# A fused attention and feed-forward kernel: the rounding of the remaining keys moves to ScalarE, and the static order of the start is redrawn

## The chip, the cores and the metric

The kernel runs on one core of a Trainium2 chip. The metric is the device time of one execution in microseconds; the kernel before took 277.38 us in the median of three runs (276.81 to 309.06). The profile comes from one profiled execution, whose span was 274.6 us. The engines are called PE (TensorE, matmuls), PEld (its weight loads), DVE (VectorE), ACT (ScalarE), POOL (GpSimd) and SP (SyncE, which issues nearly all of the transfers).

## The reference

Two blocks follow each other: a polynomial-sketch attention, and a multiplicative feed-forward network on its output.

```python
# q, k, v: (4 batches, 4 heads, 1088 rows, 32); S1, S2: (8, 32), held as float64
def phi(x):
    a = np.einsum('rd,bhsd->bhsr', S1, x)
    b = np.einsum('rd,bhsd->bhsr', S2, x)
    return np.einsum('bhsi,bhsj->bhsij', a, b).reshape(*x.shape[:-1], r * r)
q_p, k_p = (phi(q), phi(k))
kv = np.einsum('bhsf,bhsd->bhfd', k_p, v)
z = np.sum(k_p, axis=2)
num = np.einsum('bhsf,bhfd->bhsd', q_p, kv)
den = np.einsum('bhsf,bhf->bhs', q_p, z)[..., None] + 1e-06
attn = (num / den).astype(np.float32)
# x: the attention output as (4352, 128); w1, w2 (128, 1024), w3 (1024, 1024), w_out (1024, 128)
a = x @ w1
b = x @ w2
h = a * b @ w3
out = (h @ w_out).astype(np.float32)
```

The denominator needs more accuracy than one f32 product gives. The kernel therefore never sums `k_p` for it; it takes the Gram matrix of the keys, G = sum of k kᵀ, with every key split into a rounded leading part and a rest, and gets the denominator's matrix from S1, G and S2. That is the "Gram chain": Gram products, then `G`, then `T`, then `N`, then the query matrices `R`. The 1088 rows of a head are 8 chunks of 128 and 64 remaining rows; the "remaining keys" are those 64 rows of two batches, stacked on 128 partitions.

## The kernel before

The order of all instructions is fixed when the program is built. Steps are entered in a plan with engine, estimated time, what they read and write, and a rank; a list scheduler then emits them one after the other, lower rank first among those that could start at about the same time. `EARLY` holds the ranks of the first batch's steps, `FIRST` those of the rest, `PRODUCTS` how many small matmuls a step issues. Where the plan sees TensorE idle it inserts matmuls on zeros (`idle_ps`), which compute nothing that is used.

```python
def first_rest(m, g, engine):          # leading part of the remaining keys
    for x, t, rows in rest_rows(m):    # two groups of 64 partitions
        if engine is nc.vector:
            round_to(t[:, 0], x, g[rows])
            continue
        gb = bview(g[rows], [[0, H], [0, D]])
        engine.tensor_add(t[:, 0], x, gb)
        engine.tensor_sub(t[:, 0], t[:, 0], gb)

def second_rest(m, engine):            # what the leading part leaves
    for x, t, _ in rest_rows(m):
        engine.tensor_sub(t[:, 1], x, t[:, 0])

# first batch: "first_r": first_rest(0, g[0], nc.gpsimd), "second_r": second_rest(0, nc.gpsimd)

def G_rest():                          # end of G: PSUM to SBUF, then masked blocks
    gb = work.tile([128, D], F32, tag="gb", bufs=1, name="gb")
    nc.vector.tensor_sub(gb, acc["g1"], acc["ga"])
    nc.vector.tensor_add(gb, gb, acc["g2"])
    acc["G"].append(blocks("gB", gb))  # blocks: tensor_mul of two SBUF tiles

# ... (pair_steps, the rest of T)
    nc.vector.tensor_sub(b, hi, a); nc.vector.tensor_add(b, b, lo); nc.vector.tensor_add(s, a, b)

# ... key features of batch 0 on GpSimd, two halves, from b_sb in SBUF
op(f"kp{half}", "POOL", 1.92, f"kp{half}", (("w3c", "b", half),), (("kp", 0, half),))

# ... queries, group g (two groups of 512 rows to a batch)
def lead_q():                          # ScalarE
    nc.scalar.activation(s["q2"], s["qT"], ACT.Identity, bias=g)
    nc.scalar.activation(s["q1"], s["q2"], ACT.Identity, bias=g, scale=-1.0)
def rest_q():                          # "rem", GpSimd
    nc.gpsimd.tensor_add(s["q2"], s["qT"], s["q1"])
# split, dens, dens2, phi: VectorE work on 128x256 tiles, most of it with two SBUF inputs

# ... sums over the keys of batch b = 1, 2, 3 on TensorE (32-column tiles)
p.op("gs0", "PE", 0.75, st["gs0"], (("k", b), ("kk", b)), (("kvz", b),))
p.op("gs1", "PE", 1.1, lambda: run_all(st[x] for x in ("gs1", "rg")), ...)
p.op("kv0", "PE", 0.5, st["kv0"], (("kp", b, 0), ("v", b)), (("kvz", b),))
kv1 = p.op("kv1", "PE", 0.6, lambda: run_all(st[x] for x in ("kv1", "rv")), ...)

# ... feed-forward, group g, chunk c of 8: a = x w1 (PE), copy (ACT), b = x w2 (PE), a*b (DVE), o += ab (w3 w_out) (PE)
```

The feed-forward uses w3 and w_out multiplied together beforehand (`w3_t`, the transposes, and `w3_mm`); the raw float64 weights are turned to f32 by ACT (`cv_c`, `cv_m`, `sgn`) and DVE.

Of the kernel before, what the change touches and what calls it, by code (L numbers as in the profile page):

```python
# [27 lines left out]
def bview(t, free):  # L28
# [6 lines left out]
        "q2": 1, "ay": 1, "ayC": 1, "hl": 1, "pr": 1, "bs": 1, "pT": 1, "xT": 3, "oT": 2, "b_sb": 2}  # L35
SHARED = {"t", "wa", "wb", "ph", "kvz"}

COLUMNS = {"ay": 32, "ab": 32, "rg": 32, "rv": 32, "gs0": 32, "gs1": 32, "kv0": 32, "kv1": 32, "nd0": 64, "nd1": 64, "nd4": 16}

PRODUCTS = {"ay": 48, "ay2": 32, "ab": 16, "gs0": 64, "gs1": 76, "rg": 12, "rv": 4, "kv0": 32, "kv1": 36, "nd4": 64, "w3_mm": 16, "w3_t": 4}  # L40
MOST = 120
TURN = 0.1

FIRST = {"words": 1, "conv": 1.5, "early": 1.5, "k": 2, "KX": 10, "q": 0.8, "q_act": 1, "k_act": 0, "a": 2, "b": 2.1,
         "o": 0.9, "many": 6, "late": 3, "w3_t": 1, "w3_t_copy": 0, "w3_mm": 1.7, "k1": 1.3, "mul": 0.55, "wait": 0.35}

EARLY = {"tr": -9, "Pg": -8, "sT": -10, "grid": -8, "split": -10, "grid1": -2, "tr1": -7, "rem": -8.5, "rem1": -6,
         "lead": -10, "lead1": -6, "R": -7, "k_ab0": -11, "k_ab1": -6, "r_ab": -9, "r_tr": -9, "kv0": -12, "kv1": -5,
         "rv": -10, "P_mm": -12, "P_copy": -8, "P": -8, "kp0": -8, "kp1": -10, "r_kp": -8.5, "peak1": -8.5, "gs1": -12,
         "k_tr": -10, "rg": -11, "second_r": -9.5}  # L50

HELD = {"dens", "dens2", "conv", "second", "T_rest"}
LATENCY = {"PE": 0.27, "DVE": 0.2, "ACT": 0.23, "POOL": 0.3, "SP": 3.8}


class Plan:
# [36 lines left out]
    def order(self):  # L93
        ops = self.ops
        tiles = {tag: list(keys) for tag, keys in self.held.items()}
        end, left, res, clock = {}, [], [], {}
        columns = 128
        issued = []
        pool, held = [], (0.0, 0.0)
        turn = {}  # L100
        for op in ops:
            for key in op[5]:
                if key[0] not in SHARED:
                    turn.setdefault(key[0], []).append(key)
        for n, (_, engine, us, *_r) in enumerate(ops):
            if engine is None:
                end[n] = (None, us)
            else:
                left.append(n)

        def seen(n, engine):
            e, t = end[n]
            return t if e in (None, engine) and e != "SP" else t + LATENCY[e]

        while left:
            best = {}
            for i in left:
                _, engine, us, _, deps, new, rank = ops[i]
                if any(d not in end for d in deps):
                    continue  # L120
                t = max([clock.get(engine, 0.0)] + [seen(d, engine) for d in deps])
                ok = all(key[0] in SHARED or turn[key[0]][0] == key for key in new)
                for key in new:
                    before = tiles.get(key[0], [])
                    if len(before) >= BUFS[key[0]]:
                        users = self.users[before[-BUFS[key[0]]]]
                        if any(u not in end for u in users):
                            ok = False
                            break
                        t = max([t] + [seen(u, engine) for u in users])  # L130
                if engine == "PE" and COLUMNS.get(ops[i][0], 128) != columns:
                    t += TURN
                if engine == "PE":

                    room = MOST - PRODUCTS.get(ops[i][0], 2)
                    for at, count in reversed(issued):
                        room -= count
                        if room < 0:
                            t = max(t, at + (4.0 if 18 < at < 95 else 2.0 if at > 18 else 0.5))
                            break  # L140
                if ok:
                    best.setdefault(engine, []).append((t, rank(tiles, end) if callable(rank) else rank, i))
            first = None
            for engine, c in best.items():
                t0 = min(c)[0] + 0.1
                t, r, i = min((x for x in c if x[0] <= t0), key=lambda x: (x[1], x[2]))

                for x in c:
                    if x[0] <= t0 - 0.1 + FIRST["wait"] and x[1] < min(r, 0) - 0.9:
                        t, r, i = x  # L150
                if first is None or t < first[0]:
                    first = (t, i, engine)
            t, i, engine = first
            left.remove(i)
            us = ops[i][2]
            if engine == "DVE":
                if ops[i][0] in HELD:
                    us += 0.7 * sum(max(0.0, min(f, t + us) - max(s, t)) for s, f in pool[-2:])
                held = (t, t + us) if ops[i][0] in HELD else (t, t)
            elif engine == "POOL":  # L160
                pool.append((t, t + us))
                clock["DVE"] = clock.get("DVE", 0.0) + 0.7 * max(0.0, min(held[1], t + us) - max(held[0], t))
            end[i] = (engine, t + us)
            clock[engine] = t + us
            if engine == "PE":
                columns = COLUMNS.get(ops[i][0], 128)
                issued.append((t, PRODUCTS.get(ops[i][0], 2)))
            for key in ops[i][5]:
                tiles.setdefault(key[0], []).append(key)
                if key[0] not in SHARED:  # L170
                    turn[key[0]].pop(0)
            res.append((t, i))
        return res
# [3 lines left out]
def kernel(  # L177
# [249 lines left out]
    def run_all(steps):  # L427
        for f in steps:
            f()
# [263 lines left out]
            yield k_rs[m][rows], kk_rs[rows, i], rows  # L693

    def first_rest(m, g, engine):
        for x, t, rows in rest_rows(m):
            if engine is nc.vector:
                round_to(t[:, 0], x, g[rows])
                continue
            gb = bview(g[rows], [[0, H], [0, D]])  # L700
            engine.tensor_add(t[:, 0], x, gb)
            engine.tensor_sub(t[:, 0], t[:, 0], gb)

    def second_rest(m, engine):
        for x, t, _ in rest_rows(m):
# [2 lines left out]
    def lead_first():  # L708
# [14 lines left out]
        def second(part):  # L723
# [2 lines left out]
        chunks = lambda half: lambda t: t[:, :, 4 * half:4 * half + 4]  # L726
        return {"peak0": lambda: peak(0), "peak1": lambda: peak(1), "peaks": peaks,
                "first": first, "second0": lambda: second(chunks(0)), "second1": lambda: second(chunks(1)),
                "first_r": lambda: first_rest(0, g[0], nc.gpsimd), "second_r": lambda: second_rest(0, nc.gpsimd)}

    def lead(b):

# [195 lines left out]
    def k_ops(b):  # L928
# [19 lines left out]
            kp = op(f"kp{half}", "DVE", 1.15, (("ph", "k", b),), (("kp", b, half),), rank)  # L948
        if b == 2:
            rest_ops(m, kp)  # L950
        p.op("gs0", "PE", 0.75, st["gs0"], (("k", b), ("kk", b)), (("kvz", b),))
        p.op("gs1", "PE", 1.1, lambda: run_all(st[x] for x in ("gs1", "rg")), (("k", b), ("kk", b), ("kkr", m)), (("kvz", b),))
        p.op("kv0", "PE", 0.5, st["kv0"], (("kp", b, 0), ("v", b)), (("kvz", b),))
        kv1 = p.op("kv1", "PE", 0.6, lambda: run_all(st[x] for x in ("kv1", "rv")), (("kp", b, 1), ("v", b), ("kpr", m), ("vr", m)),
             (("kvz", b),))
        if b + 2 < B:
            for which in "kv":
                p.op("load", "SP", 2.0, lambda which=which: load_in(which, b + 2), (), ((which, b + 2),), 3)
        if b == 1:
            p.op("load", "SP", 0.7, lambda: load_rest(v_rs, v, 1, of_one), (), (("vr", 1),), 1, (kv1,))  # L960
        fin1 = op("fin1", "DVE", 1.7, (("kvz", b),), (("G", b),), rank)
        op("T_mm", "PE", 0.6, (("G", b),), (("t", "T", b),))
        op("T_pair", "DVE", 1.4, (("t", "T", b),), (("Tp", b),), rank)
# [216 lines left out]
    def q_ops(g):  # L1180
# [21 lines left out]
                p.op("load", "SP", 1.6, lambda: load_by_head("q", b + 2), (), (("qh", b + 2),), 3)  # L1202
        op("grid", "DVE", 0.35 + 0.6 * w, (qT,), (("gq", g),), after=begin)
        op("lead", "ACT", 0.2 + 1.2 * w, (qT, ("gq", g)), (("q1", g), ("q2", g)))
        op("rem", "POOL", 1.15, (qT, ("q1", g), ("q2", g)), (("q2", g),))
        R = [*(("R", b) for b in batches), *(("Rs", n) for n in range(4))]
        if lean:
            op("ay1", "PE", 0.25, (("q1", g), *(R if g else (("Rh", 0), ("Rs", 0)))), (("wa", "ay", g),), after=last_phi)
        else:
            p.op("ay", "PE", 0.12 + 1.2 * w, lambda: run_all((st["ay1"], st["ay2"])), (qT, ("q1", g), ("q2", g), *R),  # L1210
                 (("wa", "ay", g), ("wb", "ay", g)), 0, last_phi)
# [116 lines left out]
    def first_ops():  # L1328
# [19 lines left out]
        op("first", "DVE", 0.73, "first", (("k", 0), ("gk", 0)), (("kk", 0),))  # L1348
        op("second0", "DVE", 0.62, "second0", (("k", 0), ("kk", 0)), (("k2", 0),))
        op("second1", "DVE", 0.65, "second1", (("k", 0), ("kk", 0)), (("k2", 1),))  # L1350
        op("first_r", "POOL", 1.7, "first_r", (("kr", 0), ("gk", 0)), (("kkr", 0),))
        op("second_r", "POOL", 0.95, "second_r", (("kr", 0), ("kkr", 0)), (("kkr", 0),))
        for half in range(2):
            ps = ("h", "ab", half)
            op(f"k_ab{half}", "PE", 0.98, f"ab{half}", (("kT", 0, half), ("ST",)), (ps,))
# [14 lines left out]
        op("P_mm", "PE", 0.75, sketch_P_mm, (("pT", "s"),), (("wa", "P"),))  # L1370
        op("P_copy", "ACT", 0.2, sketch_P_copy, (("wa", "P"),), (("Pc",),))
        op("Pg", "DVE", 0.58, sketch_P_peak, (("Pc",),), (("Pg",),))
        op("P", "POOL", 1.93, sketch_P, (("Pc",), ("Pg",)), (("P",),))
        op("T_lead", "DVE", 0.9, "T_lead", (("t", "T"),), (("Tp", 0),))
        op("T_rest", "DVE", 0.55, "T_rest", (("t", "T"), ("Tp", 0)), (("Tb", 0),))
        op("N_mm1", "PE", 0.2, "N_mm1", (("Tp", 0), ("P",)), (("t", "N"),))
        op("N_mm2", "PE", 0.4, "N_mm2", (("Tb", 0), ("P",)), (("t", "N"),))
# [96 lines left out]
```

## Time and profile before

| what | value |
|---|---|
| time, median of 3 | 277.38 us |
| span of the profiled execution | 274.6 us |
| PE busy | 266.8 us (97%) in 2556 matmul records |
| DVE busy | 208.8 us (76%) |
| ACT busy | 122.7 us (45%) |
| POOL busy | 21.4 us (8%) in 31 instructions |
| matmuls on zeros | 55 records, 13.8 us busy |
| TensorE clock granted | 1.00 in all but the last stretch |

Busy time is the union of the records of an engine. The matmuls overlap each other in the pipeline, so the time that one adds is read from the distance between the starts of consecutive ones: the two records of one f32 128x512 product take 1.02 us in the timeline, but the next product starts 0.86 us after it. The last stages of the profile show how long the start lasts: the first feed-forward matmul starts 32.13 us into the span.

### The profile page before, as it was taken

What the parts mean: (1) busy time and instruction counts of PE and PEld (TensorE: products, weight loads), DVE (VectorE), ACT (ScalarE), POOL (GpSimd) and SP (SyncE); (2) the same over time, 40 slices, a digit from 0 to 9 for tenths busy, and PEclk for the clock granted to TensorE, in tenths of its full rate; (3) what the DMA queues carried; (4) which work ended last, traced back from release to release, by engine and by line L of the source; (5) the groups of instructions that cost most, each with busy time, mean ns of one, the idle gap of its engine ahead of it and who ended that gap; (6) DMA issues with size and microseconds to landing.
All of it is one profiled execution on the core that took longest, in us unless ns stands there. A gap on an engine that the chain in (4) does not pass through costs nothing.

```text
span 274.6 us, 6300 instructions
## 1 busy us (share of the span) xinstructions
PE 266.8 (97%) x2556; PEld 150.6 (55%) x2556; DVE 208.8 (76%) x507; ACT 122.7 (45%) x265; POOL 21.4 (8%) x31
## 2 busy tenths in 40 slices
PE   7999999998999999999999999999999999999995
PEld 2865634476774767645454446454444444444665
DVE  7999999999999999995648699847795585583231
ACT  4783977997866982111232240224123222323120
POOL 2772001000000010000010010001000100000000
PEclk9999999999999999999999999999999999999999
DMA  4759999579820210020200200020002002000103
GB/s 138 271 127 314 280 383 221 183 205 304 242 78 21 79 63 2 2 39 2 38 2 0 40 0 5 0 40 2 0 0 41 0 2 38 2 0 11 31 0 57
DMA packets 28876, 22.42 MB, mean 82 GB/s; under 512 B 20016, under 2 KB 25392, under 8 KB 28848
## 3 DMA queue, kind: packets, MB, share of 16 engines
q1 hardware_dynamic: 28704, 21.96, 29.2%
q8 instruction: 20, 0.33, 0.5%
q10 hardware_dynamic: 144, 0.07, 0.1%
q14 instruction: 8, 0.07, 0.1%
HBM read 19.80 MB, written 2.23 MB: 80 GB/s over the span
## 4 chain that ended last, share of the span: by engine, by line
PE 83%; DVE 11%; DMA 2%; ACT 2%; issue 1%; DVEq 0%; ACTq 0%
PE ps_o L1292 21%; PE b_ps L1273 19%; PE a_ps L1263 19%; PE ps_w3o L577 5%; PE ps_kvz L775 3%; PE ps_wt L565 3%; PE ps_c L1034 2%; DMA raw<-in_moe_w_dram 2%; PE idle_ps L358 2%; PE ps_o L1288 1%; PE ps_xt L1156 1%; PE ps_ab L672 1%; DVE ph L1109 1%; DVE w L424 1%; DVE qT L1173 1%
## 5 line engine op out<-in xcount | busy, mean ns | idle before, releaser
L1268 ACT COPY ffa<-a_ps 128x512 f32<-128x512 f32 (+1 forms) x72 | 40.5, 563 | 104.1 <-PE a_ps L1263 104.0
L1278 DVE TENSOR_TENSOR ab<-ffa,b_ps 128x512 f32<-128x512 f32 (+1 forms) x72 | 46.6, 649 | 41.3 <-PE b_ps L1273 38.5
L1273 PE MATMUL b_ps<-xT,w 128*128 128x512 f32 (+1 forms) x144 | 71.1, 575 | 0.0
L1263 PE MATMUL a_ps<-xT,w 128*128 128x512 f32 (+1 forms) x144 | 70.6, 572 | 0.1
L1292 PE MATMUL ps_o<-ab,w3o 128*128 128x512 f32 x128 | 65.6, 604 | 0.0
L1273 PEld LDWEIGHTS b_ps<-xT,w 128*128 128x128 f32 x144 | 26.1, 190 | 29.1 <-issue 24.3
L1263 PEld LDWEIGHTS a_ps<-xT,w 128*128 128x128 f32 x144 | 26.3, 190 | 27.2 <-issue 19.8
L1292 PEld LDWEIGHTS ps_o<-ab,w3o 128*128 128x128 f32 x128 | 22.8, 190 | 21.0 <-issue 19.0
L1007 POOL TENSOR_TENSOR q<-qT,q 128x512 f32<-128x512 f32 x8 | 9.6, 1194 | 184.9 <-ACT q L1003 181.4
L375 ACT CAST sgn<-cv_c 128x512 f16<-128x512 f32 x22 | 17.2, 782 | 0.0
L577 PE MATMUL ps_w3o<-wo,w3T 128*128 128x128 f32 x128 | 15.8, 275 | 1.0 <-issue 1.0
L577 PEld LDWEIGHTS ps_w3o<-wo,w3T 128*128 128x128 f32 x128 | 15.1, 192 | 1.6 <-issue 1.3
L358 PE MATMUL idle_ps<-zeros 128*128 128x448 bf16 x55 | 13.8, 396 | 1.8 <-DVE zeros L352 1.8
L411 ACT ACTIVATE cv_c<-raw 128x512 f32<-128x512 f32 x22 | 15.3, 696 | 0.0
L414 ACT ACTIVATE cv_m<-raw 128x512 int32<-128x512 uint32 x22 | 15.2, 692 | 0.0
L424 DVE CUSTOM_DVE_ANT_0 w3c<-w3c,cv_m 128x1024 uint16<-128x1024 uint16 x16 | 11.9, 743 | 0.4
L1109 DVE TENSOR_TENSOR ph<-ay,bs 128x512 f32<-128x512 f32 (+1 forms) x12 | 11.1, 948 | 0.2
L421 DVE SCALAR_TENSOR_TENSOR w3c<-cv_c,sgn 128x512 int32<-128x512 int32 x16 | 10.9, 683 | 0.3 <-ACT sgn L375 0.3
L565 PEld LDWEIGHTS ps_wt<-ident,w3c 128*128 128x128 f32 x64 | 7.7, 144 | 6.0 <-issue 2.8
L572 ACT COPY w3T<-ps_wt 128x512 f32<-128x512 f32 x16 | 9.5, 595 | 2.1 <-PE ps_wt L565 1.7
L358 PEld LDWEIGHTS <-zeros 128*128 128x128 bf16 x55 | 5.7, 109 | 7.7 <-issue 2.9
L565 PE MATMUL ps_wt<-ident,w3c 128*128 128x128 f32 x64 | 9.8, 276 | 0.0
(213 smaller groups left out, 354.5 us busy)
## 6 DMA issues: line engine op xcount, KB each, us to landing
raw<-in_moe_w_dram SPq DMA_DIRECT2D x20, 512.0 KB, 6.4
qh<-in_q_dram SPq DMA_DIRECT2D x4, 544.0 KB, 7.2
out_dram<-oT SPq DMA_DIRECT2D x33, 64.0 KB, 2.0
k_sb<-in_k_dram SPq DMA_DIRECT2D x4, 512.0 KB, 8.1
kh<-in_k_dram SPq DMA_DIRECT2D x12, 128.0 KB, 4.0
v_sb<-in_v_dram SPq DMA_DIRECT2D x12, 128.0 KB, 7.0
raw<-in_moe_w_out_dram SPq DMA_DIRECT2D x2, 512.0 KB, 7.4
v_sb<-in_v_dram SPq DMA_DIRECT2D x1, 512.0 KB, 5.1
```

What stands on the lines that cost most here:

```text
L358: nc.tensor.matmul(ps[:, :448], zeros[:, :128], zeros, start=True, stop=True)
L375: nc.scalar.copy(bview(t.bitcast(F16)[:, 1:], [[2, n]]), c)
L411: nc.scalar.mul(x["c"], halves(raw[n], CW)[1].bitcast(F32), 2.0 ** -112)
L414: nc.scalar.mul(x["m"].bitcast(I32), halves(raw.pop(n), CW)[0].bitcast(U32), 2.0 ** -29)
L424: nc.vector.tensor_tensor(x["t"], x["t"], x["m"].bitcast(I32), ALU.add)
L565: nc.tensor.transpose(ps[i][:, c], w3c[i][:, c * 128:(c + 1) * 128], ident)
L577: nc.tensor.matmul(ps["mm"], w3T[ko][:, c], wo[:, c], start=(c == 0), stop=(c == NC - 1))
L1263: nc.tensor.matmul(a_sb[g, c, "ps"][:, :n], w1[:, c * 128:(c + 1) * 128], xT[key], start=True, stop=True)
L1268: nc.scalar.copy(a_sb[g, c][:, :n], a_sb.pop((g, c, "ps"))[:, :n])
L1273: nc.tensor.matmul(ab_sb[g, c, "ps"][:, :n], w2[:, c * 128:(c + 1) * 128], xT[key], start=True, stop=True)
L1278: nc.vector.tensor_mul(ab_sb[g, c][:, :n], a_sb.pop((g, c))[:, :n], ab_sb.pop((g, c, "ps"))[:, :n])
L1292: nc.tensor.matmul(o_ps[g][:, :n], w3o[:, c], ab_sb.pop((g, c))[:, :n], start=c == 0, stop=c == NC - 1)
```

## The change

It does five things, all for the order in which the start and the key sums run:

1. The leading part of the first batch's remaining keys is rounded by ScalarE (one negation of the grid and four activations with a bias) instead of GpSimd (two additions and two subtractions).
2. The ranks of the first batch's steps are redrawn so that the Gram products come before the key features on TensorE, and the sketch matrix P before the key features on GpSimd; the second query group's peak goes behind the first group's `phi`.
3. The second query group's rest (`rem`) may start only after its first product `ay1`, which puts it beside `split` instead of beside the first group's `phi`.
4. For batches 2 and 3 the Gram sums are one step, and the key-value sums are one step, so that nothing is put between their halves.
5. The plan's own rules change: three more VectorE steps count as held up by GpSimd, the limit on small matmuls is dropped after 95 us of planned time, and `FIRST` ranks `b` before `o`.

The rest of the diff makes the list scheduler itself faster on the host and changes no instruction.

```diff
-PRODUCTS = {..., "gs0": 64, "gs1": 76, ...}
+PRODUCTS = {..., "gs": 140, "kv": 68, "gs0": 64, "gs1": 76, ...}
-FIRST = {..., "a": 2, "b": 2.1, "o": 0.9, ..., "w3_t_copy": 0, ...}
+FIRST = {..., "a": 2, "b": 1.9, "o": 1.95, ..., "w3_t_copy": 0.3, ...}
-EARLY = {..., "sT": -10, "grid1": -2, "tr1": -7, "rem": -8.5, "lead": -10, "k_ab0": -11, "k_ab1": -6, "r_ab": -9,
-         "kv0": -12, "P": -8, "kp0": -8, "kp1": -10, "k_tr": -10, "second_r": -9.5, ...}
+EARLY = {"first_r": -13, "k_tr_copy": -12.5, ..., "sT": -9.2, "grid1": -7, "tr1": -7.5, "rem": -11, "lead": -11,
+         "k_ab0": -6, "k_ab1": -5.9, "r_ab": -5.5, "kv0": -5, "P": -12, "kp0": -5, "kp1": -5, "k_tr": -12,
+         "second_r": -12, "gs0": -12, "b_copy": -9, "ay2": -10, "ay1": -11, ...}
-HELD = {"dens", "dens2", "conv", "second", "T_rest"}
+HELD = {"dens", "dens2", "conv", "second", "T_rest", "phi", "second0", "second1"}
@@ (scheduler)
-                    for at, count in reversed(issued):
+                    for at, count in reversed(issued if t < 95 else ()):
@@
     def first_rest(m, g, engine):
+        if engine is nc.scalar:
+            minus = work.tile([128, 1], F32, tag="g_minus", bufs=1, name="g_minus")
+            engine.mul(minus, g, -1.0)
+            for grid, first in ((g, True), (minus, False)):
+                for x, t, rows in rest_rows(m):
+                    engine.activation(t[:, 0], x if first else t[:, 0], ACT.Identity, bias=grid[rows])
+            return
         for x, t, rows in rest_rows(m):
-            if engine is nc.vector:
-                round_to(t[:, 0], x, g[rows])
-                continue
-            ... (the two GpSimd operations)
+            round_to(t[:, 0], x, g[rows])
-                "first_r": lambda: first_rest(0, g[0], nc.gpsimd), ...
+                "first_r": lambda: first_rest(0, g[0], nc.scalar), ...
@@ (sums over the keys)
+        if b == 1:
+            ... (gs0, gs1, kv0, kv1 as before)
+        else:
+            p.op("gs", "PE", 1.75, lambda: run_all(st[x] for x in ("gs0", "gs1", "rg")), reads, (("kvz", b),))
+            kv = p.op("kv", "PE", 1.1, lambda: run_all(st[x] for x in ("kv0", "kv1", "rv")), ...)
@@ (queries)
-        op("rem", "POOL", 1.15, (qT, ("q1", g), ("q2", g)), (("q2", g),))
+        def rem(after=()):
+            op("rem", "POOL", 1.15, (qT, ("q1", g), ("q2", g)), (("q2", g),), after=after)
+        if g != 1:
+            rem()
...
+            if g == 1:
+                rem((ay1,))
```

What the plan makes of it, in the order of the instructions: on DVE the copy and masking of the sketch (`ST`, `S12blk`) move from ahead of the keys' rounding to behind it, and the second query group's transposes and peak move back; on PE the four feature products of batch 0's first half move behind the Gram products, with four matmuls on zeros in their old place; on POOL both halves of the key features stand behind P, one directly after the other. The first feed-forward products stand ahead of the second query group's `ay2` instead of behind it. There are 51 matmuls on zeros instead of 55 in all; of the ones after the first feed-forward product there were three, and there are none.

## The prediction

> **What bounds the kernel now.** I read the page's busy times and its chain of waits first, then the timeline of TensorE alone, then VectorE and GpSimd side by side over the first 30 us. The page says that matmuls carry the end:
>
> ```profile
> PE 266.8 (97%) x2556; PEld 150.6 (55%) x2556; DVE 208.8 (76%) x507; ACT 122.7 (45%) x265; POOL 21.4 (8%) x31
> ...
> PE 83%; DVE 11%; DMA 2%; ACT 2%; issue 1%; DVEq 0%; ACTq 0%
> ```
>
> A busy PE is a weak sign, as records overlap, so the timeline of PE counts: start, duration, what. From its first feed-forward product on, one product starts 0.86 us after the last whatever it is:
>
> ```profile
> 32.13 1.02 PE L1263 MATMUL a_ps<-xT,w 128*128 128x512 f32 x2
> 33.00 1.02 PE L1273 MATMUL b_ps<-xT,w 128*128 128x512 f32 x2
> 33.85 1.02 PE L1263 MATMUL a_ps<-xT,w 128*128 128x512 f32 x2
> 34.71 1.02 PE L1273 MATMUL b_ps<-xT,w 128*128 128x512 f32 x2
> 35.57 0.35 PE L358 MATMUL idle_ps<-zeros 128*128 128x448 bf16 x1
> 35.78 1.13 PE L1263 MATMUL a_ps<-xT,w 128*128 128x512 f32 x2
> ...
> 205.49 1.02 PE L1263 MATMUL a_ps<-xT,w 128*128 128x512 f32 x2
> 206.44 0.31 PE L1156 MATMUL ps_xt<-phiT,kz 32*32 32x128 f32 x4
> ```
>
> So the kernel is two parts: a start of 32.1 us, bound by VectorE's chain, and 240 us in which TensorE hardly pauses. What the second part loses is small: three matmuls on zeros (0.21, 0.19 and 0.44 us), turns between 128- and 32-column tiles (the last product above stays 0.95 instead of 0.86 us), and one pause in the chain of waits, called issue:
>
> ```profile
> 65.10 0.67 PE ps_w3o L577 x6
> 65.77 1.01 issue
> 66.78 1.27 PE ps_w3o L577 x10
> ```
>
> The start is read from GpSimd and VectorE together:
>
> ```profile
> 15.80 1.96 POOL L656 TENSOR_TENSOR kp<-b_sb 128x1024 f32<-128x1024 f32 x1
> 16.91 0.87 DVE L464 TENSOR_TENSOR Ts<-Ta,Tb 128x8 f32<-128x8 f32 x1
> ...
> 24.98 1.15 POOL L1007 TENSOR_TENSOR q<-qT,q 128x512 f32<-128x512 f32 x1 [3.47 <-DVE rc L1096]
> 25.54 1.75 DVE L1109 TENSOR_TENSOR ph<-ay,bs 128x512 f32<-128x512 f32 x2
> ```
>
> Ts adds eight columns and lasts 0.87 us, ending when GpSimd's kp does (17.76); without GpSimd the same line takes 0.17 us in batch 1. The two ph take 1.75 us, 1.29 us for the second group. VectorE waits for GpSimd's read, and everything behind it moves. (The bracket is the idle time before, and who ended it.)
>
> [...] Ts and ph wait, while the reads of PSUM inside kp (Ta 0.28, Tb 0.17 us) do not. [...] The trace shows 0.09 to 0.1 us at most such turns.
>
> **The change part by part.** I took the new order of instructions from the built kernel, and put the old durations to it; these are hand sums, not measurements.
>
> *Keys' rounding.* The grid is ready at 7.90 us in both. Before, ST and S12blk (7.96 to 8.46) came next, then kk waited for GpSimd's 8.46 to 8.85 and ended at 9.40; the two second halves took turns with GpSimd and ended at 11.01. After: kk needs about 0.55 (9.40 minus 8.85), so 7.95 to 8.50, and the halves 0.6 each, so 9.7. That is 1.3 us gained on VectorE, of which 0.5 is only S12blk moved back. ScalarE does the negation and four activations at the 0.21 us spacing of its L526 group with one dependent wait: about 1.2 us, done at 9.2. GpSimd's two subtractions (0.39 each) wait for the half in progress, 9.7 to 10.5.
>
> *Gram sums.* The key transposes leave PE at 8.8; four matmuls on zeros (0.77 us before) make the Gram products start at 9.6 instead of 10.26. They take 1.53 us plus 0.35 for the rests: the features start at 11.5, and G's peak follows at 11.8 instead of 12.96. Gain here: 1.15 us.
>
> *Where it is given back.* From peak to the masked block gB the old chain takes 1.59 us, so gB comes at 13.4. The features take 0.13 x 8 us, 0.34 to ScalarE, 0.43 for its two copies and 0.08 to GpSimd, so kp0 starts at about 13.25, by a hair earlier. gB reads two SBUF tiles: it then waits for kp0's 1.95 us until 15.2 and ends at 15.5, the q peak adds 0.97, T starts at 16.5, and Ts, 1.22 us later, is done at 17.9. If gB wins instead, kp0 and kp1 run from 13.7 to 17.6, T starts at 14.6, and Ts, due at 15.85, waits until 17.6. Both ways end at 17.7 to 17.9, against 17.78 before. The two kp stand one behind the other, and VectorE must cross them once. N then starts after the moved transposes (0.75 us) at about 18.5, against 18.67, while the second group's peak (0.97 us), done before at this point, is still owed.
>
> *Split, dens and phi.* The second group's rest no longer blocks ph: minus 0.46 us. But the remaining keys' feature (0.63 us on GpSimd), before at 20.89 beside a PSUM read, now follows six weight activations on ScalarE (18.9 to 22.4) and a small chain on PE, and lands at about 23.4, inside dens, whose inputs are all in SBUF: plus 0.5. So phi ends near 27.1 (27.3 before), the owed peak follows, and the two first weights are joined at 30.8 instead of 29.94. ScalarE's query lead ends at 30.2, the attention output's copy at 30.75. PE then does ay1, one a, one b and ay2, and stands at 34.55 where it stood at 33.85. The start loses 0.7 us.
>
> *The long part.* The three matmuls on zeros go: minus 0.84. I counted the turns between tile widths from the first feed-forward product on, in both orders: 44 before, 36 after, for the merged sums and for other order; eight at 0.1 are minus 0.8. The 1.01 us issue pause stands behind two bursts of small matmuls (88 and 72 ps_kvz records) and moves with the order; I count half of it, 0.5, and another 0.1 for w3o's later place.
>
> Sum: +0.7 - 0.84 - 0.8 - 0.6 = -1.5 us, from 277.4 to 275.9.
>
> **The rivals.**
> [...] If the real order lets gB through and Ts between the two kp, the 1.15 us of the Gram chain survive, and the owed peak costs nothing because VectorE is ahead. For it: the redrawn ranks were made for this chain, and the plan now counts more steps as held. Against it: kp0 and kp1 leave no hole, and Ts falls in them by more than a microsecond on either way. It would make 274 to 274.5.
> Second, TensorE's time is only renamed. VectorE is 92 to 99% busy in nearly every 10 us from 20 to 120; where zeros are taken out PE would just wait for VectorE's product of a and b, and where VectorE arrives 0.9 us late all of that stays. For it: the busy time by stretch (9.76 of 10 at 40 to 50, 9.90 at 50 to 60). Against it: PE has no larger pauses there, so VectorE keeps up. It would make 277 to 278.
> Third, merged sums cost a pause of their own: 152 records in one go (the largest after the start was 120, and that group took 2.32 us at 108.9 against 1.68 at 168.6). Twice 0.6 would take back the turns. It would make about 277.
> Fourth, the gate for the next loads sits behind gB: if gB waits, the loads leave at 16.5 instead of 15.6. Keys of batch 1 are read at 29.9 and land early enough in the old trace; I expect nothing from it, at worst 1 us.
>
> **Range and chances.** The middle is 275.9. The first rival is the good end and the second with the third the bad one; a sum of parts under 1 us each with signs of both kinds is worth about 2 us to either side, so 273.8 to 278.0. A gain over 2% would need 5.5 us: more than every part together, as 97% of the span is matmuls that stay. I give it 0.05, a loss of 2% 0.03, and 0.92 to within 2%.
>
> **What would show it.** Right: kk's rounding about 0.55 us long and G's peak near 11.8; gB or Ts as long as a kp; N's peak near 18.5; the first feed-forward product near 31; no zeros after it; 0.86 us spacing to the end with fewer 0.95s. Wrong: Ts at 0.17 us and N's peak before 17.7 (first rival); gaps between feed-forward products from 32 to 60 us (second); a pause behind the merged sums near 109 and 168 us (third); VectorE waiting for the keys of batch 1 (fourth). The prediction fails in size if the long part, which I take as fixed but for 2.2 us, changes by more.

## The result: 280.1 us against 277.1 us, and the profile after

The changed kernel takes 280.07 us (median of four, 279.75 to 280.33), the kernel before 277.10 us in the runs beside it. The ratio is 1.0112, with an interval of 1.0088 to 1.0136: slower by about 1.1%, where 275.9 us was predicted. The span of the profiled execution grew from 274.6 to 277.9 us.

From the page of the changed kernel: busy time of each engine, and the clock that TensorE was granted in 40 slices:

```profile
PE 268.7 (97%) x2552; PEld 151.7 (55%) x2552; DVE 209.4 (75%) x507; ACT 125.2 (45%) x270; POOL 19.9 (7%) x27
...
PEclk9968999999999999999999999999999999999999
```

The first line looks harmless: 97% as before, with four matmuls fewer. But it holds 1.9 us more of busy time, so the matmuls became slower. The clock row tells where: its third and fourth slices (13.9 to 27.8 us) read 6 and 8, where the row of the kernel before has full speed. Next the timeline of the changed kernel in those slices, TensorE (start, duration, line, output and inputs; the bracket is the idle time before):

```profile
15.45 0.39 PE L484 MATMUL ps_T<-ST,gB 128*128 128x8 f32 x2 [1.42 <-DVE gB L848]
15.69 3.01 PE L370 MATMUL idle_ps<-zeros 128*128 128x448 bf16 x9
18.49 0.43 PE L482 MATMUL ps_N<-Ta,P 128*128 128x8 f32 x2
...
36.37 1.05 PE L1290 MATMUL a_ps<-xT,w 128*128 128x512 f32 x2
```

and the lines of VectorE and GpSimd in the same timeline:

```profile
13.57 1.82 DVE L848 TENSOR_TENSOR gB<-gb,mask 128x128 f32<-128x128 f32 x1
...
17.58 0.17 DVE L476 TENSOR_TENSOR Ts<-Ta,Tb 128x8 f32<-128x8 f32 x1
...
13.29 3.91 POOL L668 TENSOR_TENSOR kp<-b_sb 128x1024 f32<-128x1024 f32 x2 [0.23 <-ACT b_sb L660]
```

(gB is the masked second part of G, Ts the sum of T's two parts; N's peak, below, is the reduction with which VectorE starts on N; kp0 and kp1 are the two halves of the key features.) GpSimd's two kp run without a hole from 13.29 to 17.20. gB comes 0.28 us after the first one began and ends 0.15 us behind it, as predicted; Ts, without a kp beside it, takes 0.17 us. What was not predicted stands on TensorE: it waits 1.42 us for gB, and the nine matmuls on zeros behind the wait take 3.01 us, where eleven took 2.24 us before. In the timeline of the kernel before:

```profile
15.24 2.24 PE L358 MATMUL idle_ps<-zeros 128*128 128x448 bf16 x11
```

The table by stretch of the changed kernel (length, busy time of PE, PEld, DVE, ACT and POOL with the count of instructions, then the granted clock, DMA share and GB/s) shows why:

```profile
15.00:16.00 1.00, 0.55 (x4) 0.44 (x5) 0.99 (x2) 0.00 (x0) 1.00 (x2) 1.00 0.00 0
16.00:17.00 1.00, 1.00 (x6) 0.40 (x3) 0.83 (x7) 0.60 (x1) 1.00 (x1) 0.62 0.00 0
17.00:18.00 1.00, 1.00 (x4) 0.46 (x3) 0.90 (x5) 0.97 (x4) 0.25 (x2) 0.50 0.48 102
...
23.00:24.00 1.00, 1.00 (x11) 1.00 (x10) 0.93 (x3) 0.00 (x0) 0.00 (x0) 0.96 1.14 399
```

From 16.25 to 23.08 us the clock is exactly half. N's products (18.49), the feature sums and the query products up to the first split (22.01) all run in this stretch.

The second place is in the long part. The chain of waits of the changed kernel, at batch 3's merged sums:

```profile
169.19 2.67 PE ps_kvz L789 x172
171.86 1.24 issue
173.10 0.47 PE ps_kvz L789 x17
```

In the same view of the kernel before these sums took 3.07 us in three pieces (0.70, 1.68 and 0.69); here they take 4.38 us in one, 1.24 us of them a stop for which the profile shows no wait.

Two marks divide the loss. When the second query group's products ay1 and ay2 and one a and one b of the feed-forward are done, TensorE stands at 36.37 us instead of 33.85 (this is called the mark below): the start lost **2.52 us**. From there to the start of the last product it takes 238.26 us instead of 237.49: the long part lost **0.77 us**.

### The profile page after: what moved, and what is told of

Read it like the earlier page. It is cut to its first block, busy times and chain, and to the rows that moved or that the text cites. A ratio compares the mean times of both kernels' runs of the same rounds, so it can differ in the third digit from the quotient of the medians.

```text
span 277.9 us, 6294 instructions
## 1 busy us (share of the span) xinstructions
PE 268.7 (97%) x2552; PEld 151.7 (55%) x2552; DVE 209.4 (75%) x507; ACT 125.2 (45%) x270; POOL 19.9 (7%) x27
## 4 chain that ended last, share of the span: by engine, by line
PE 75%; DVE 14%; DMA 3%; issue 3%; ACT 3%; SPq 0%; DVEq 0%; ACTq 0%
PE ps_o L1319 20%; PE b_ps L1300 18%; PE a_ps L1290 17%; PE ps_w3o L589 3%; DMA v_sb<-in_v_dram 3%; PE ps_kvz L789 3%; PE ps_wt L577 2%; PE ps_c L1055 2%; DVE ab L1305 1%; PE ps_o L1315 1%; PE ps_xt L1177 1%; PE ps_ab L684 1%; DVE w3c L433 1%; PE idle_ps L370 1%; DVE kk L763 1%
## 5 line engine op out<-in xcount | busy, mean ns | idle before, releaser
L1319 PE MATMUL ps_o<-ab,w3o 128*128 128x512 f32 x128 | 63.2, 603 | 0.0
L1028 POOL TENSOR_TENSOR q<-qT,q 128x512 f32<-128x512 f32 x8 | 10.2, 1276 | 185.6 <-ACT q L1024 104.9
L436 DVE CUSTOM_DVE_ANT_0 w3c<-w3c,cv_m 128x1024 uint16<-128x1024 uint16 x16 | 11.0, 690 | 0.4
```

The source lines that it names most:

```text
L1319: nc.tensor.matmul(o_ps[g][:, :n], w3o[:, c], ab_sb.pop((g, c))[:, :n], start=c == 0, stop=c == NC - 1)
```

## The experiments

The theory after this reading: (A) in the start, the pause of TensorE behind the held gB halves its clock, and that, not the hold itself, is most of the 2.5 us; (B) in the long part, the merged sums of batch 3 cost a stop of their own. The rivals: the rounding on ScalarE is what delays the start; the hold costs by its length alone; the stop was there before and only moved.

All edits keep the plan's order except for what they name. `seq` is the planned order, and `at(name, which)` finds a step in it:

```python
seq = p.order()
at = lambda name, which: [x for x, (_, i) in enumerate(seq) if p.ops[i][0] == name][which]
```

Ratios are to the kernel before on the same chip. The pause is the largest sum of TensorE's idle time within 3.41 us in the profiled execution, between 12 and 22 us of the span, so that stops later in the kernel are not in it (3.41 us is the shortest stretch at half clock in these profiles, from 172.71 to 176.12 us in "rounding on GpSimd"); the last column counts the runs with a mean clock under 0.996 (6.83 us at half clock is a mean of 0.988).

| kernel | what it does | median us | ratio, interval | pause us | under 0.996 |
|---|---|---|---|---|---|
| before | | 277.1 | 1 | 0.64 | 35 of 155 |
| changed | | 280.07 | 1.0112 (1.0088 to 1.0136) | 1.42 | 4 of 4 |
| copy later | gB freed | 277.65 | 1.0054 (1.0032 to 1.0075) | 1.02 | 8 of 22 |
| zeros in the wait | A alone, gB still held | 278.37 | 1.0046 (1.0018 to 1.0073) | 0.48 | 0 of 8 |
| sums apart | B alone | 277.65 | 1.0046 (1.0026 to 1.0066) | 1.41 | 11 of 15 |
| rounding on GpSimd | part 1 undone | 279.97 | 1.0120 (1.0084 to 1.0156) | 1.29 | 6 of 6 |
| burst in the old kernel | B put into before | 278.51 | 1.0067 (1.0046 to 1.0087) | 1.06 | 2 of 13 |
| one product apart | half of B | 278.97 | 1.0074 (1.0054 to 1.0095) | 1.42 | 12 of 13 |
| both edits | copy later, sums apart | 276.11 | 0.9976 (0.9962 to 0.9990) | 1.70 | 4 of 22 |
| peak early | and the peak moved | 276.65 | 0.9982 (0.9960 to 1.0005) | 1.16 | 15 of 22 |
| kp later by one copy | and one copy | 275.30 | 0.9953 (0.9929 to 0.9976) | 1.23 | 6 of 17 |
| kp later by three | and three copies | 277.15 | 1.0000 (0.9977 to 1.0024) | 1.56 | 13 of 14 |
| zeros in two waits | one copy, pauses filled | 274.83 | 0.9929 (0.9904 to 0.9953) | 0.20 | 0 of 9 |
| both causes on the spot | A and B alone | 276.60 | 0.9991 (0.9976 to 1.0007) | 0.48 | 0 of 22 |

### Copy later: gB freed from kp0

```diff
+    seq.insert(at("b_copy", 0), seq.pop(at("R", 2)))   # ScalarE's Rl work ahead of the first feature copy
```

> The changed kernel with one edit: on ScalarE, four Rl activations stand before the first half's feature copy instead of behind it, so the first kp on GpSimd starts about 0.85 us later (14.15 instead of 13.30), after gB has run. Nothing else moves. Theory [...]: gB lasts 0.3 to 0.4 us instead of 1.82, the granted clock stays 1.0 from 10 to 30 us, N's peak comes at 17 to 17.5 us instead of 19.82, the first feed-forward product at 30.5 to 31.5 instead of 32.89, and the time falls by 1.5 to 2.5 us from 280.1, to about 278. Rival (the five slower operations on ScalarE, 0.43 us apart, are the loss): the keys' rests still come as late, and the time stays within 0.4 us of 280.1.

kp0 starts at 14.08 instead of 13.29. The timeline of this kernel:

```profile
13.50 0.29 DVE L848 TENSOR_TENSOR gB<-gb,mask 128x128 f32<-128x128 f32 x1
...
15.97 0.17 DVE L476 TENSOR_TENSOR Ts<-Ta,Tb 128x8 f32<-128x8 f32 x1
...
14.09 1.86 PE L370 MATMUL idle_ps<-zeros 128*128 128x448 bf16 x9
```

gB takes 0.29 us, the nine zeros 1.86 instead of 3.01, and Ts slips in ahead of kp1. N's peak is at 16.98 instead of 19.82, and the mark at 33.56, ahead of the kernel before. The ratio falls by 0.0058. So in this profile the loss of the start is gone with the hold on gB; the run does not yet tell the hold from the clock, and 8 of its 22 runs still fell under 0.996.

### Zeros in the wait: the hold stays, the pause goes

```diff
         def T_mm2():
+            if b == 0:
+                idle(8)
             pair_mm_steps(acc["ps"], *acc["G"], S1aT, S1bT, S1sT)[2]()
```

> The changed kernel with eight matmuls on zeros put between T's second and third product on TensorE, that is into the 1.4 us in which it stands waiting for gB. gB stays held by kp. Theory: the halved clock is a separate, second part of the loss, set off by that pause. The granted clock stays 1.0 from 16 to 23 us, N's peak comes at about 18.5 instead of 19.82 and the first query split at about 20.8 instead of 22.0, so the time falls by 1.0 to 1.7 us. Rival (VectorE's chain alone sets the start, the clock matters little there): gain under 0.3 us.

The timeline of this kernel, VectorE's gB and TensorE:

```profile
13.52 1.83 DVE L848 TENSOR_TENSOR gB<-gb,mask 128x128 f32<-128x128 f32 x1
...
13.84 1.67 PE L370 MATMUL idle_ps<-zeros 128*128 128x448 bf16 x8
15.41 0.39 PE L484 MATMUL ps_T<-ST,gB 128*128 128x8 f32 x2
15.65 1.86 PE L370 MATMUL idle_ps<-zeros 128*128 128x448 bf16 x9
```

gB is held just as long (1.83 us), and its product starts at 15.41 as in the changed kernel (15.45). But the clock stays at 1.00, the next nine zeros take 1.86 us, and N's peak comes at 18.49 instead of 19.82. The mark is at 34.38: of the 2.52 us lost in the start, 1.99 are gone with eight matmuls whose result nobody uses. This separates (A) from the rival: at full clock and with gB held, the start loses 0.53 us against the kernel before. (The hold itself costs more: "copy later", also at full clock in its profile, has its mark 0.82 us earlier, at 33.56.)

Part of this gain is lost again behind the mark. The long part takes 239.20 us here, 0.94 more than in the changed kernel, with a stop of 1.45 us in batch 3's sums. The profiled run is the slowest of the eight.

### Sums apart: batch 3's feature sums behind the next o, a and b

```diff
+    kv = at("kv", -1)
+    b = next(x for x in range(kv, len(seq)) if p.ops[seq[x][1]][0] == "b")
+    seq.insert(b, seq.pop(kv))
```

> The changed kernel with three feed-forward products (an o, an a and a b) moved between batch 3's Gram sums and its key-value sums, which the change had put one behind the other. Theory (the 1.24 us pause at 171.9 us, called issue, comes from the length of the burst of small matmuls): the pause goes, two more turns cost 0.2 to 0.3 us, and the time falls by 0.7 to 1.1 us. Rival (the pause is a wait for the features or values of batch 3, which ends at 173 us whatever stands before): the pause shrinks only by what the moved products cover, and then the time would fall as well, but the sums would show an idle time that a semaphore ended; if it is caused by the number of small matmuls in all and not by their density, the pause only moves and the time stays within 0.3 us.

The chain of waits of this kernel:

```profile
169.96 1.75 PE ps_kvz L789 x117
...
174.47 1.14 PE ps_kvz L789 x72
```

The stop is gone: the sums are 1.75 and 1.14 us, together 2.89 instead of 4.38. The long part takes 236.73 us, 1.53 less, which is more than the 0.7 to 1.1 us expected. The pause behind gB is untouched (1.41 us), and in the profiled execution the clock was halved even for 10.24 us (17.14 to 27.38). So (B) can be taken away without (A), and each alone is worth 0.0066 of the ratio.

### Rounding on GpSimd: is ScalarE's new work to blame?

```diff
-                "first_r": lambda: first_rest(0, g[0], nc.scalar), ...
+                "first_r": lambda: first_rest(0, g[0], nc.gpsimd), ...   # with the two additions and subtractions back
```

> The changed kernel, its order kept, with the first rounding of the remaining keys back on GpSimd (two additions, two subtractions). Theory [...]: kk's rounding takes 1.0 instead of 0.82 us, and its halves take turns with GpSimd again, so VectorE is 0.5 to 0.8 us later at the G peak; gB is still held by kp, so the later chain is about the same and the time is 0 to 0.8 us longer than 280.1. Rival (ScalarE's rounding is the loss): the time falls by 1 us or more.

No: 1.0120. In this order kp0 came 0.5 us later (13.83), gB won with 0.41 us, and Ts lost instead. The timeline:

```profile
16.20 1.56 DVE L476 TENSOR_TENSOR Ts<-Ta,Tb 128x8 f32<-128x8 f32 x1
...
17.91 0.36 PE L484 MATMUL ps_N<-Ts,P 128*128 128x8 f32 x2 [0.97 <-DVE Ts L476]
```

TensorE waits 0.97 us here, and the clock is halved from 19.11 to 25.94. It is halved a second time in this profile, from 172.71 to 176.12, right behind the stop in batch 3's sums, which is 1.74 us long here (170.37 to 172.11). So in this execution (B) seems to have brought on the half clock too. Which of the two VectorE instructions kp holds matters less than that TensorE stands still behind it.

### Burst in the old kernel, and one product apart: what the stop is

In the kernel before, batch 3's four steps put directly behind each other; then, in the changed kernel, a single output product put between the Gram and the feature sums:

```diff
+    for name in ("gs1", "kv0", "kv1"):                       # kernel before
+        x = seq.pop(at(name, -1))
+        seq.insert(at({"gs1": "gs0", "kv0": "gs1", "kv1": "kv0"}[name], -1) + 1, x)
```
```diff
+    kv = at("kv", -1)                                        # changed kernel
+    o = next(x for x in range(kv, len(seq)) if p.ops[seq[x][1]][0] == "o")
+    seq.insert(o, seq.pop(kv))
```

> The kernel before, with batch 3's four key-sum steps put one behind the other (the b, a and o that stood between them come after them). Nothing else moves. Theory (burst): a pause of 0.8 to 1.5 us called issue appears inside these sums and the time grows by 0.4 to 1.0 us, as two to four turns of 0.1 us are saved. Rival (merging is good in itself and the pause was due to something else in the changed kernel): the time falls by 0.2 to 0.4 us.

> The changed kernel with a single feed-forward product (o, 0.86 us) between batch 3's Gram sums and its key-value sums. If the pause is a debt of time (small matmuls are used up faster than they are supplied), one product pays 0.86 us of the 1.24: a pause of 0.2 to 0.5 us stays and the time falls by 0.4 to 0.9 us. If it is a fixed stop once some number of small matmuls has gone by without a break, one product removes all of it and the time falls as with three products apart (by about 1.2 us in the long part).

The chain of waits of the kernel before with the burst:

```profile
165.19 2.54 PE ps_kvz L775 x203
167.73 1.67 issue
169.40 0.53 PE ps_kvz L775 x21
```

and of the changed kernel with one product between:

```profile
170.19 1.05 PE ps_o L1319 x2
171.24 0.91 PE ps_kvz L789 x53
172.15 0.44 issue
172.59 0.53 PE ps_kvz L789 x19
```

The old kernel, untouched otherwise, gets the stop and loses 0.0067, or 1.9 us, more than the 0.4 to 1.0 us expected. One product of 1.05 us in between leaves 0.44 of 1.24 us. So the stop is no fixed price of a merged step. It behaves like a debt that longer work pays back: the 1.05 us took 0.80 us off it.

What the stops go together with can be read from the same traces. The page of the changed kernel counts, among the DMA queues, packets of a kind called instruction (how many, megabytes, share of the DMA engines), and the other pages count as many:

```profile
q8 instruction: 20, 0.33, 0.5%
```

Each of them has 16384 bytes. Number TensorE's 5152 to 5168 records (weight loads, matmuls and a few waits) in the order of their starts, from 0. The first record behind the stop in batch 3's sums is number 3777 in all six kernels that have it, although the steps around it differ: changed, copy later, zeros in the wait, rounding on GpSimd, burst in the old kernel, one product apart. The pause called issue in the kernel before (1.01 us at 65.77) stands ahead of record 1473, and a smaller one of 0.38 us at 110.41, in batch 2's sums, ahead of record 2497. These numbers are 1024 and 1280 apart, both multiples of 256. And each of these stops ends 1.2 to 1.6 us after one of the packets has landed: in the changed kernel a packet lands at 171.74 and the sums go on at 173.10. With the sums apart, record 3777 is due only 2.15 us after a landing, and nothing stops. A count of small matmuls fits less well: the stop comes after 164 to 203 of them in batch 3, and after 99 in batch 2 of the kernel before. And "zeros in the wait", which has eight matmuls (16 records) more ahead of the sums than the changed kernel, stops eight matmuls earlier in them, after 164 instead of 172.

That TensorE stands still there because the next block of its instructions has not come is my reading. Every stop read here agrees with it, but no run changed the packets themselves, so it is not shown. What the traces show is the place: in all six kernels with the stop in batch 3's sums it falls ahead of record 3777, wherever in the run of small matmuls that record stands.

### Both edits, peak early, kp later: looking for the better version

The two edits together; then also the second query group's peak moved back to before N; then one or three copies of one element on ScalarE ahead of the first feature copy, to move kp0 and kp1 away from gB and Ts:

```diff
+    grid1 = seq.pop(at("grid", 1))
+    seq.insert(at("N_rest", 0), grid1)
```
```diff
+            def b_copy(half=half):
+                for _ in range(1 * (half == 0)):      # 3 in the second version
+                    nc.scalar.copy(first_act, mask4[:1, :1])
+                st[f"b_copy{half}"]()
```

> The changed kernel with two of the edits together: the first half's feature copy behind the Rl activations, so that gB runs before kp, and batch 3's sums apart. If the loss has exactly two places, the start (2.5 us at equal work) and the burst (1.2 us), both gains add: the work that stood at 36.4 us stands at about 33.5, the last product starts near 270.5 instead of 274.6, and the time is 0.2 to 0.5% below the kernel before (ratio 0.995 to 0.998). If they share a cause (one shift that moves waits about), the sum gives no more than the better of them, ratio 1.004.

> As the kernel with both edits, and the second query group's peak (0.97 us on VectorE) moved from behind the first group's phi to a place right behind Rh, where VectorE stands about 0.75 us waiting for GpSimd's query rest with Rf. Theory: half of the peak hides in that wait, so VectorE reaches the first weights 0.4 to 0.6 us earlier and the time falls by 0.2 to 0.6 us more, ratio 0.993 to 0.997. Rival (TensorE is by then held by ScalarE's query lead and output copy, not by the weights): no change against the kernel with both edits.

> The kernel with both edits and the early peak, and one copy of a single element on ScalarE ahead of the first half's feature copy, which starts the first kp 0.1 to 0.2 us later. [...] in the profile with both edits Ts lost, lasted 1.96 us and the clock was halved; with the early peak it won. Theory (this race makes the times spread over 274.7 to 278.2 us): Ts now asks before the first kp ends, lasts about 0.2 us in the profile, and the times close up near 275, ratio 0.993 to 0.996. Rival (the spread is the chip's): spread and median stay, ratio 0.998.

> The same with three such copies: the first kp 0.3 to 0.6 us later. Race theory: Ts always wins the gap between the two kp, but waits for it 0.2 to 0.4 us longer than with one copy, so the times are as close together and 0.1 to 0.4 us longer, ratio 0.994 to 0.997.

"Both edits" beats the kernel before by a little. In its profiled execution Ts at 15.88 lost against kp1 at 15.86 and took 1.96 us; with the peak early, Ts at 16.07 was ahead of kp1 at 16.11 and took 0.17 us. A race decided within 0.04 us is no design. In the median the early peak brought nothing (0.9982 against 0.9976, where 0.2 to 0.6 us had been expected): 15 of its 22 runs are under 0.996. One copy gives 0.9953. Three copies miss what was expected: kp1 is then out of the way, but TensorE waits longer for it. The timeline with three copies, TensorE:

```profile
18.59 0.65 PE L789 MATMUL ps_kv<-kp,v_sb 128*32 128x64 f32 x32 [0.85 <-POOL kp L668]
...
20.07 0.61 PE L1066 MATMUL ps_c<-Rf,q 128*128 128x64 f32 x2 [0.61 <-DVE Rl L891]
```

Two pauses, neither long, and the clock is halved from 20.14 us in the profile, and for as much in 13 of 14 runs. With one copy they are 0.48 and 0.68 us, and 6 of 17 runs have a mean clock under 0.996: those six have a median of 276.69 us, the other eleven 274.81.

### Zeros in two waits, and both causes on the spot

If the sum of pauses is the cause, filling them must remove both the loss and the spread:

```diff
+        if n == seq[at("kv1", 0)][1]:      # on top of "kp later by one copy"
+            idle(2)
+        if n == seq[at("ay2", 0)][1]:
+            idle(3)
```

> The version with one copy ahead of the features, with two matmuls on zeros ahead of the second half of the first batch's feature sums and three ahead of the first query products: TensorE's two pauses of 0.48 and 0.68 us at 17.5 and 18.9 us are filled, nothing else moves. If the halved clock follows from the sum of TensorE's pauses within some 3.4 us (1.23 us there, and 6 of 17 runs had a mean clock below 0.996), that sum falls to about 0.2 us, the mean clock is 1.00 in nearly every run, and the median is that of the runs at full clock, 274.8 us, ratio 0.992 to 0.994. If the halving has another cause that TensorE's pauses only accompany, about a third of the runs stay below 0.996 and the ratio stays near 0.9953.

> The changed kernel with both named causes taken away where they stand, without touching the order of the start: eight matmuls on zeros in TensorE's wait for gB, and batch 3's feature sums behind the next o, a and b. gB stays held by kp0 (1.8 us). If the two causes are separate and explain the loss, the gains add: 1.0112 - 0.0066 - 0.0066 = 0.998, with the clock at 1.00, the second ay2 done near 34.4 us and a long part near 236.7 us. If they share a cause, or the clock halves elsewhere, the ratio is between 1.002 and 1.005.

The timeline of the first of them, TensorE:

```profile
17.46 0.55 PE L370 MATMUL idle_ps<-zeros 128*128 128x448 bf16 x2
18.00 0.65 PE L789 MATMUL ps_kv<-kp,v_sb 128*32 128x64 f32 x32
...
18.71 0.73 PE L370 MATMUL idle_ps<-zeros 128*128 128x448 bf16 x3
19.56 0.41 PE L1066 MATMUL ps_c<-Rf,q 128*128 128x64 f32 x2
```

The work behind the zeros starts at the same times as without them (18.00 and 19.56), no run has a halved clock, and the median is 274.83 us, ratio 0.9929: the lowest median of all, though its interval still touches that of the version without these zeros. "Both causes on the spot" is the changed kernel with the eight zeros and the sums apart, everything else as the change has it: 0.9991. Taking away (A) and (B) adds up (0.998 was expected) and leaves no measurable difference to the kernel before. The two causes are the loss, and without them the change brings nothing either.

## Why the prediction was wrong, step by step

**Two steps failed.** The predicted sum was minus 1.5 us. In the profiles the start lost 2.52 us where 0.7 was predicted, 1.8 too much, and the long part lost 0.77 us where a gain of 2.2 was predicted, 3.0 too much.

**The first is "Where it is given back"**, and with it the sum of the start. It counted what VectorE and GpSimd do to each other, and let TensorE take its old durations. gB held to 15.2 to 15.5 was right (15.39 measured), and so was Ts done at 17.7 to 17.9 (17.75). Then N's peak, predicted near 18.5, came at 19.82, since TensorE had stood still for 1.42 us and ran at half clock behind it. With the pause filled and nothing else changed, N's peak is at 18.49, the first feed-forward product at 30.91 (predicted near 31), and the start loses 0.53 us (predicted 0.7). So the mechanism of the start was right as far as it went; the missing term, the clock, measured 1.99 us.

**The second is "The long part"**, which booked zeros, turns and the issue pause as time saved. Waits for VectorE and a longer issue pause took their place.
- The third rival came true at one of its two places. At 168 us the predicted pause is there, 1.24 us instead of the 0.6 that I gave it. At 109 us there is none: the two merged steps of batch 2 do not follow each other, as the Gram sums run at 104.68 and the key-value sums at 122.24.
- The second rival came true too. The zeros (0.84 us) and the old issue pause (1.01) did go, but by the distance of starts three new waits of 0.34, 0.32 and 0.98 us came in at 55.8, 57.4 and 100.5 us. The longest, in the timeline of the changed kernel:

```profile
102.33 0.63 PE L577 MATMUL ps_wt<-ident,w3c 128*128 128x128 f32 x4 [0.82 <-DVE w3c L436]
```

From 95.8 to 101.6 us that kernel's chain of waits lies on VectorE nearly throughout. So TensorE's time was largely renamed there, as the rival said.
- The prediction counted one issue pause in the kernel before. There is a second, the 0.38 us at 110.41, and it went as well. Minus 0.84, minus 1.01, minus 0.38, plus 1.64, plus 1.24 make plus 0.65; measured were plus 0.77. For the eight turns (0.8) and w3o's place (0.1) this rough account leaves no gain, where I had 0.9. No run tested the turns alone.
- Without the stop in batch 3's sums ("both causes on the spot") the long part is 236.97 us, 0.52 less than before, against the predicted 2.2.

**Right, or nearly:**
- G's peak at 11.8: 11.88. The way there was not as drawn. kk took 0.82 us instead of 0.55, and ScalarE's rounding 1.8 us instead of 1.2: its four activations have 128 elements to a partition and come 0.43 us apart, while the 0.21 us was read from activations of 32. The second did not set the end: with the rounding back on GpSimd the peak comes at 11.97.
- The second group's rest no longer blocks ph: the two take 1.29 us instead of 1.75. The remaining keys' feature does land in dens and costs 0.31 us there instead of 0.5. The owed peak follows phi at 29.01, and with TensorE's pause filled phi ends at 27.11 (predicted near 27.1).
- The fourth rival, later loads, has no sign in the trace: batch 1's keys are read at 32.64 us without a wait.

The first rival, in which gB gets through and Ts falls between the two kp, describes the better versions, not this kernel: with gB and Ts both free ("copy later", 0.29 and 0.17 us) N's peak is at 16.98, before the 17.7 that was named as its sign.

The range ended at 278.0. Two losses took the time to 280.07: 1.99 us without any term in the sum, and 1.24 us counted only as a rival and at half its size. With either one taken away the ratio is 1.0046, or about 278.4 us, still just outside.

Not tried: the second group's rest behind ay1 alone, batch 2's merged step alone, and the new ranks one by one. Why VectorE is late at 55 and 100 us stays open.

## What to carry to other kernels

When a change makes TensorE wait, ask not only who is late but also what the clock does behind the wait: here 1.4 us of idle time in the start cost 2 us more through the clock, and matmuls on zeros in the wait, which delayed nothing (gB's product at 15.41 instead of 15.45 us), took it back. A plan that fills idle time by its own estimates misses the waits that its estimates miss; put the zeros where the trace shows the pause. And after merging small matmuls into one long run, look in the chain of waits for a stop called issue: here it was 1.24 us, one large product between them shortened it to 0.44 us, and three removed it.

## What the runs showed of the hardware

- **Half clock after short pauses.** The halved stretches of these traces are 3.41, 6.83 or 10.24 us long. A single pause of 1.41 or 1.42 us in the start went with a lowered mean clock in 27 of 32 runs of three kernels, and two pauses of 0.85 and 0.61 us in 13 of 14. From 0.64 to 1.23 us it happened in some runs of each kernel, and with at most 0.48 us in the start in none of 39. The length of the pause does not decide alone: the stop of 1.45 us at 170 us in "zeros in the wait" halved the clock in none of its 8 runs, and with 1.67 us at 168 us in "burst in the old kernel" 2 of 13 are under 0.996, while half clock did follow the 1.74 us in the profile of "rounding on GpSimd". Products of 512 columns follow soon behind those stops, products of 8 columns and zeros behind the pause in the start; whether that is the reason, no run tested. The half clock began 0.80 us behind the end of the pause in the changed kernel (15.45 to 16.25), 1.34 us behind it with the sums apart (15.80 to 17.14), and 1.20 us with the rounding on GpSimd (17.91 to 19.11); what sets this distance, no run tested either. Where the profiled execution is not typical the table can mislead: "both edits" shows 1.70 us, but its profile is one of the four runs with a halved clock.
- **Stops at the same record.** Stops called issue stand directly ahead of records 1473, 2497 and 3777 of TensorE and end 1.2 to 1.6 us after a 16384-byte packet of the queue called instruction has landed. In batch 3's merged sums they lasted 1.24 to 1.74 us in five kernels, and 0.44 us with one large product between.
- **Whoever starts first holds the other.** gB took 0.29 us ("copy later") and 0.41 us ("rounding on GpSimd") where it started ahead of kp0, and 1.82 us in the changed kernel, where kp0 was 0.28 us ahead: it ended 0.15 us behind kp0. Ts took 0.17 us where no kp ran or where it started just ahead of kp1, and 0.87 us (before), 1.56 us ("rounding on GpSimd") and 1.96 us ("both edits") behind a kp that had started. In the first two of these it ended 0.02 us behind that kp.
